# Attention block with modulated layer norm: scale product in three parts, last output columns gated on VectorE

## The chip, the cores and the metric

The kernel runs on one core of one Trainium2 chip. The metric is the device time of one execution in microseconds (us), as a median of several runs. The core's engines work side by side, each through its own queue in order: TensorE (PE in the profile; PEld are its weight loads), VectorE (DVE), ScalarE (ACT), GpSimd (POOL) and SyncE (SP), which here issues most DMAs. An engine starts an instruction when all that stands before it in its own queue is issued and the semaphores that it waits for are set.

## The reference

```python
B, N, D = (2, 256, 1152)
mod = (_silu(c) @ w_mod).reshape(B, 6, 1, D)
shift_a, scale_a, gate_a, shift_m, scale_m, gate_m = [mod[:, i] for i in range(6)]
h = _layernorm(x, axis=-1) * (1 + scale_a) + shift_a
qkv = h @ wqkv
q, k, v = (qkv[..., :D], qkv[..., D:2 * D], qkv[..., 2 * D:])
p = _softmax(jnp.einsum('bqd,bkd->bqk', q, k) * D ** (-0.5), axis=-1)
a = jnp.einsum('bqk,bkd->bqd', p, v) @ wo
return x + gate_a * a
```

All inputs are bf16. x is [2, 256, 1152], c [2, 1152], wqkv [1152, 3456], wo [1152, 1152], w_mod [1152, 6912], of which the first three sixths (shift, scale, gate) are used.

## The kernel before

The 512 tokens of both batches are four tiles of 128 (t = 0 to 3; two tiles a batch), and D is nine tiles of 128 (k). All weights are loaded once.

*Who sets the order.* `vec`, `sca`, `ten` and `spq` (L81 to L84) record each instruction for DVE, ACT, PE and SP; `pin` (L86) then fixes those four queues to the order in which the source calls them. POOL is not pinned. So a line moved in the source moves in its engine's queue, and everything behind it in that queue waits for it. All recorded instructions carry line 74; they are told apart by their tiles' names.

*Loads* (L149 to L164, all issued by SP): x tiles 1, 0, 3; the first CA = 384 columns of `wS` (scale) in five pieces; the first 1024 columns of K's first two weight slices; x tile 2; the third slice; the other 768 columns of `wS` in three pieces of 576 KB; the other slices of `wK` in four pieces; the left-over columns of the first three; `wH` (shift). The weights of Q, V, the gate (`wG`) and `wO` follow.

*Start of the work* (L342 on). Thirteen filler matmuls on `junk_ps` keep TensorE busy while the first tiles arrive. Tile 1's mean comes from DVE (`dve_stats`, `dve_aggr`), the others' from ACT (`act_mean`). `centre(t)` (L224, DVE) writes x less its mean to `xc`; `turned` (L228) transposes its 128-column blocks on TensorE into psum; `from_psum` copies them to `xnT`. The variance of tiles 0 and 2 comes from ACT (`act_var`), that of 1 and 3 from DVE's `bn_stats`. The 1/sigma of a token isn't applied here: POOL computes it (`var_eps` L211, `rstd_parts` L249) as three bf16 parts, TensorE turns and spreads it over the partitions (`rstd_turn`, `rstd_spread`), and it is multiplied in later.

*Scale.* `scale_A` (L282) multiplies silu(c) with the first three column tiles of `wS`, into `psS0` and `psSA`; `scale_B` (L289) does the other six, into `psSB`. Each runs over nine row blocks kk. DVE reads the result from psum into `s1p` and writes `hTs` = `xnT` times the scale (`scaled`, L306).

*K from the scaled rows.* Six psum banks `accs` collect six of K's nine output tiles. For k = 0, 1, 2 this is done piece by piece as tokens become ready (`k_part`, L309: batch 0 first, then tile 3, then tile 2), for k = 3 to 8 for all 512 tokens (`k_step`, L323, six matmuls each). Two more output tiles take their first three k in `early_half` (L316; psum tile `psE`), and the rest later. The small psum pools `psum_a` and `psum_b` have one bank each, which `psE`, `tp3`, `tp2`, `tp8`, `psSA`, `psSB`, `turn_ps` and `spread_ps` use in turn. `tp8` holds the ninth column blocks of tiles 3 and 2. After the K steps come the shift product (`shift_block`, `psH`), the rest of K, `hT` (`modulated`), Q, the scores, V (`v_group`), and attention times V.

*Gate.* DVE sums `gacc` over the rows of `wG`; POOL's all-reduce (L589) spreads it to `gate_bc`.

*Output.* For each token tile, chunks of 384 columns are multiplied by `wO` on TensorE; DVE multiplies by the gate (`ga`) and adds x (`o_sb`); SP stores the tile. The last tile's chunks are 384, 384, 192, 128 and 64 columns. For the last 192 columns POOL has multiplied `wO` by the gate ahead of time (`wo_last`, L610); DVE then adds only x to the 128, and for the last 64 TensorE adds x by a matmul with the identity, and ACT copies them out. The three stores of the last tile hold 768, 320 and 64 columns.

Of the kernel before, what the change touches and what calls it, by code (L numbers as in the profile page):

```python
# [8 lines left out]
ALU = mybir.AluOpType  # L9
# [7 lines left out]
def kernel(  # L17
# [22 lines left out]
    NEARLY = 2  # L40
    WE = (NACC + NEARLY) * P
    KA = 3
    KB = KT - KA
    NR = 54

    x_f = x.rearrange("b n d -> (b n) d")
# [94 lines left out]
    def load_mod(tile_, which, k0, k1, c0, c1):  # L141
        spq.dma_start(out=tile_[:, k0:k1, c0:c1], in_=wmod_v[:, k0:k1, which, c0:c1])

    def load_k(k0, k1, c0=0, c1=D):
        spq.dma_start(out=wK[:, k0:k1, c0:c1], in_=wqkv_v[:, k0:k1, D + c0 : D + c1])
# [9 lines left out]
    load_k(1, 2, 0, WE)  # L155
    load_x(2)
    load_k(2, 3, 0, WE)
    for k0 in range(0, KT, 3):
        load_mod(wS, 1, k0, k0 + 3, CA, D)
    for k0, k1 in ((3, 4), (4, 5), (5, 7), (7, 9)):  # L160
        load_k(k0, k1)
    load_k(0, KA, WE, D)
    for k0, k1 in PAIRS:
        load_mod(wH, 0, k0, k1, 0, D)  # L164
# [5 lines left out]
    def fillers(n):  # L170
        for _ in range(n):
            ten.matmul(junk_ps, lhsT=junk_rhs[:, 0:P], rhs=junk_rhs, start=True, stop=True)
# [18 lines left out]
    def sc_rhs(kk):  # L191
        return scT_rep[:, kk].rearrange("p r b -> p (r b)")
# [18 lines left out]
    def var_eps(t):  # L211
        nc.gpsimd.tensor_scalar(out=rstd[:, t : t + 1], in0=mv[:, t, 1:2], scalar1=1.0, scalar2=EPS,
                                op0=ALU.mult, op1=ALU.add)
# [10 lines left out]
    def centre(t, c0=0, c1=D):  # L224
        vec.tensor_scalar(out=xc[:, t, c0:c1], in0=x_sb[:, t, c0:c1], scalar1=mv[:, t, 0:1], scalar2=None,
                          op0=ALU.subtract)

    def turned(tp, cols):  # L228
        for j, (t, k) in enumerate(cols):
            ten.transpose(tp[:, j, :], xc[:, t, k * P : (k + 1) * P], ident)  # L230

    def tiles_of(t, k0, k1):
        return [(t, k) for k in range(k0, k1)]

    def from_psum(eng, t, k0, k1, tp, j0=0):
        dst, srct = xnT[:, k0:k1, t * P : (t + 1) * P], tp[:, j0 : j0 + k1 - k0, :]
        if eng is vec:
            vec.tensor_copy(out=dst, in_=srct)
        else:
            sca.copy(out=dst, in_=srct)  # L240
# [41 lines left out]
    def scale_A(kk):  # L282
        for j in range(KA):
            ten.matmul(
                psS0 if j == 0 else psSA[:, j - 1, :], lhsT=wS[:, kk, j * P : (j + 1) * P], rhs=sc_rhs(kk),
                start=False, stop=(kk == KT - 1), skip_group_check=True,
            )

    def scale_B(kk):  # L289
        for j in range(KA, KT):  # L290
            ten.matmul(
                psSB[:, j - KA, :], lhsT=wS[:, kk, j * P : (j + 1) * P], rhs=sc_rhs(kk),
                start=(kk == 0 and j == KA), stop=(kk == KT - 1), skip_group_check=True,
            )

    def shift_block(kk):
        for j in range(KT):
# [5 lines left out]
    def one(t):  # L303
        return slice(t * P, (t + 1) * P)
# [4 lines left out]
    def k_part(k, sl, first=False):  # L309
        for f in range(NACC):  # L310
            ten.matmul(
                accs[f][:, sl], lhsT=wK[:, k, f * P : (f + 1) * P], rhs=hTs[:, k, sl],
                start=first, stop=False, skip_group_check=True,
            )

    def early_half(k, b, ps):  # L316
        for i in range(NEARLY):
            ten.matmul(
                ps[:, i, :], lhsT=wK[:, k, (NACC + i) * P : (NACC + i + 1) * P], rhs=hTs[:, k, tok(b)],
                start=(k == 0 and i == 0), stop=(k == KA - 1), skip_group_check=True,  # L320
            )

    def k_step(k):  # L323
        for f in range(NACC):
            ten.matmul(
                accs[f], lhsT=wK[:, k, f * P : (f + 1) * P], rhs=hTs[:, k, :],
                start=False, stop=(k == KT - 1), skip_group_check=True,
            )
# [16 lines left out]
    dve_stats(1, 2)  # L345
    dve_aggr(1)
    centre(1)
    var_eps(1)
    act_mean(0)
    centre(0)  # L350
    act_mean(3)
# [8 lines left out]
    from_psum(vec, 1, KA, KT, tp1b)  # L360
    scale_A(0)
    scale_A(1)
    fillers(2)
    scale_A(2)
    scale_A(3)
    turned(tp0a, tiles_of(0, 0, KA))
    turned(tp0b, tiles_of(0, KA, KT))
    from_psum(vec, 0, 0, KA, tp0a)
    from_psum(sca, 0, KA, KT, tp0b)
    for kk in range(4, KT):  # L370
        scale_A(kk)
    act_var(0)
    centre(3, 0, CW)

    accs = [psum.tile([P, T], F32, tag="mm", name="acc") for _ in range(NACC)]
    scaled(0, tok(0), psS0[:, 0:1])
# [4 lines left out]
    psE = psum_a.tile([P, NEARLY, N], F32, tag="pa")  # L381
    k_part(0, tok(0), first=True)
    early_half(0, 0, psE)
    centre(3, CW, D)
    k_part(1, tok(0))
    act_mean(2)
    tp3 = bank(n=KT - 1, pool=psum_b, tag="pb")
    turned(tp3, tiles_of(3, 0, KT - 1))
    from_psum(vec, 3, 0, KA, tp3)
    from_psum(sca, 3, KA, KT - 1, tp3, KA)  # L390
    for k in range(KA):
        scaled(k, one(3), s1p[:, k, 1:2])
    centre(2)
    early_half(1, 0, psE)
    k_part(2, tok(0))
    k_part(0, one(3))
    k_part(1, one(3))
    act_var(2)
    tp2 = bank(n=KT - 1, pool=psum_b, tag="pb")
    turned(tp2, tiles_of(2, 0, KT - 1))  # L400
    k_part(2, one(3))
    early_half(2, 0, psE)
    sca.copy(out=early[:, :, tok(0)], in_=psE)
    from_psum(vec, 2, 0, KA, tp2)
    for k in range(KA):
        scaled(k, one(2), s1p[:, k, 1:2])
    from_psum(sca, 2, KA, KT - 1, tp2, KA)
    for s in range(NCH):
        dve_stats(3, s)
    dve_aggr(3)  # L410
    var_eps(3)
    for k in range(KA):
        k_part(k, one(2))
    psSB = psum_a.tile([P, KB, NR], F32, tag="pa")
    for kk in range(6):
        scale_B(kk)
    tp8 = bank(n=2, pool=psum_b, tag="pb")
    turned(tp8, [(3, KT - 1), (2, KT - 1)])
    from_psum(vec, 3, KT - 1, KT, tp8, 0)
    from_psum(vec, 2, KT - 1, KT, tp8, 1)  # L420
    rstd_parts()
    for kk in range(6, KT):
        scale_B(kk)
    vec.tensor_scalar_add(out=s1p[:, KA:KT, :], in0=psSB[:, :, 0:B], scalar1=1.0)
    for k in range(KA, KT):
        for b in range(B):
            scaled(k, tok(b), s1p[:, k, b : b + 1])
    psE = psum_b.tile([P, NEARLY, N], F32, tag="pb")
    for k in range(KA):
        early_half(k, 1, psE)  # L430
    sca.copy(out=early[:, :, tok(1)], in_=psE)


    k_step(KA)
    rstd_turn()
    k_step(KA + 1)
    rstd_spread()
    for k in range(KT):
        vec.tensor_tensor(out=xnT[:, k, :], in0=xnT[:, k, :], in1=rstd_bc, op=ALU.mult)
    for k in range(KA + 2, KT):  # L440
        k_step(k)
    for f in range(NACC):
        evac(1, qkT[:, KT + f, :], accs[f])
# [162 lines left out]
    LASTW = 64  # L606
    TAILW = CW // 2
    wo_last = const.tile([P, KT, TAILW], BF16)
    for k in range(KT):
        nc.gpsimd.tensor_tensor(out=wo_last[:, k, :], in0=wO[:, k, D - TAILW :],  # L610
                                in1=gate_bc[:, B - 1, D - TAILW :], op=ALU.mult)
    for b in range(B):
        for gi, dv0 in enumerate(range(0, KT, 2)):
            ndv = min(2, KT - dv0)
# [10 lines left out]
    for t in range(TT):  # L625
        b = t // NQ
        o_sb = work.tile([P, D], BF16, tag="o_sb")
        if t < TT - 1:
            chunks = [(oc * CW, CW) for oc in range(NCH)]
            dma_after = {NCH - 1: (0, D)}  # L630
        else:
            chunks = [(0, CW), (CW, CW), (2 * CW, CW - TAILW), (D - TAILW, TAILW - LASTW), (D - LASTW, LASTW)]
            dma_after = {1: (0, 2 * CW), 3: (2 * CW, CW - LASTW), 4: (D - LASTW, LASTW)}
        for ci, (c0, w_) in enumerate(chunks):
            cs = slice(c0, c0 + w_)
            last = (t == TT - 1) and (ci == len(chunks) - 1)
            pregated = (t == TT - 1) and c0 >= D - TAILW
            ps = psum.tile([P, w_], F32, tag="mm")
            if last:
                ten.matmul(ps, lhsT=ident, rhs=x_sb[:, t, cs], start=True, stop=False)  # L640
            for k in range(KT):
                ten.matmul(
                    ps, lhsT=attnT[:, k, t * P : (t + 1) * P],
                    rhs=(wo_last[:, k, c0 - (D - TAILW) : c0 - (D - TAILW) + w_] if pregated else wO[:, k, cs]),
                    start=(k == 0 and not last), stop=(k == KT - 1),
                )
            if last:
                sca.copy(out=o_sb[:, cs], in_=ps)
            elif pregated:
                vec.tensor_tensor(out=o_sb[:, cs], in0=ps, in1=x_sb[:, t, cs], op=ALU.add)  # L650
            else:
                ga = work.tile([P, CW], F32, tag="ga")
                vec.tensor_tensor(out=ga[:, :w_], in0=ps, in1=gate_bc[:, b, cs], op=ALU.mult)
                vec.tensor_tensor(out=o_sb[:, cs], in0=ga[:, :w_], in1=x_sb[:, t, cs], op=ALU.add)
            if ci in dma_after:
                d0, dw = dma_after[ci]
                dma_eng = nc.scalar if last else spq
                dma_eng.dma_start(out=out_f[t * P : (t + 1) * P, d0 : d0 + dw], in_=o_sb[:, d0 : d0 + dw])
# [35 lines left out]
```

## Time and profile before

| | us |
|---|---|
| median of 3 runs (lowest, highest) | 99.31 (99.2, 99.7) |
| the profiled execution's own time | 99.89 |
| its span, first to last recorded instruction | 98.2 |
| TensorE busy | 92.7 |
| VectorE busy | 71.0 |
| ScalarE busy | 34.0 |
| GpSimd busy | 26.3 |

The times that the prediction works with are those of the profiled execution, counted from its span's start. A row of the timeline gives the start, the time from the first start to the last end, the engine, the line, the operation, out<-in by the program's names, the shape, how many instructions the row merges, and in brackets the engine's idle time before the row and what ended it. A matmul's duration holds its way through the array as well; matmuls that follow each other start closer than their durations. The granted clock is 9 tenths or more in all 40 slices, and the DMA engines are busy for nine tenths or more from 2.5 us to 52 us, at 370 to 414 GB/s from 7 us on.

### The profile page before, as it was taken

How to read it: one execution, taken by the hardware profiler on the slowest of the kernel's cores; microseconds unless marked ns; L12 is line 12 of the kernel's file. 1: busy time of each engine (PE TensorE's matmuls, PEld its weight loads, DVE VectorE, ACT ScalarE, POOL GpSimd, SP SyncE). 2: the span in 40 equal slices, each digit the busy share in tenths (PEclk: the TensorE clock that was granted, in tenths of full speed). 3: DMA queues.
4: the chain of work that ended last, by engine and by line, in shares of the span. 5: the costliest groups of instructions: out<-in, count | busy, mean ns of one | idle time of the engine just before them, and what ended most of it. 6: DMA issues, size and time to landing. Idle time of an engine off the chain costs nothing.

```text
span 98.2 us, 1836 instructions
## 1 busy us (share of the span) xinstructions
PE 92.7 (94%) x739; PEld 56.1 (57%) x739; DVE 71.0 (72%) x137; ACT 34.0 (35%) x68; POOL 26.3 (27%) x32
## 2 busy tenths in 40 slices
PE   3999999989999999999999999999999999999970
PEld 1328888634466444444448765556678755556660
DVE  1487468846955899999991999991237667879870
ACT  5195985202290792233222436332126400000000
POOL 6042001820000000000000000008999970049800
PEclk9999999999999999999999999999999999999999
DMA  2999999999999999999998000000000000302113
GB/s 48 348 295 385 387 401 404 394 411 403 384 391 387 398 408 372 372 369 365 400 414 317 33 0 0 0 0 0 0 0 7 0 0 0 120 7 114 72 67 108
DMA packets 16488, 21.06 MB, mean 215 GB/s; under 512 B 1504, under 2 KB 10976, under 8 KB 16480
## 3 DMA queue, kind: packets, MB, share of 16 engines
q1 hardware_dynamic: 16064, 20.93, 58.4%
q8 instruction: 6, 0.10, 0.4%
q10 hardware_dynamic: 416, 0.02, 0.3%
q14 instruction: 2, 0.02, 0.0%
HBM read 19.76 MB, written 1.18 MB: 213 GB/s over the span
## 4 chain that ended last, share of the span: by engine, by line
PE 87%; DVE 5%; POOL 3%; issue 1%; DVEq 0%
PE ps L74 61%; PE acc L74 10%; PE junk_ps L74 6%; PE s_ps L74 4%; PE tp L74 2%; PE psH L74 2%; DVE stats L74 1%; POOL rstd L250 1%; DVE o_sb L74 1%; DVE hTs L74 1%; DVE ga L74 1%; PE psSA L74 1%; POOL parts L251 1%; POOL parts L253 1%; DVE junk_rhs L74 1%
## 5 line engine op out<-in xcount | busy, mean ns | idle before, releaser
L589 POOL PARTITION_ALL_REDUCE gate_bc<-gacc x2 | 13.7, 6886 | 46.4 <-DVE gacc L74 46.4
L74 DVE SCALAR_TENSOR_TENSOR gacc<-wG,scT_f,gacc 128x1152 f32<-128x1152 bf16 x16 | 22.7, 1417 | 0.5
L74 PE MATMUL ps<-wqv,hT 128*128 128x384 bf16 x108 | 17.9, 326 | 0.0
L74 PE MATMUL ps<-hT,wqv 128*128 128x512 bf16 x81 | 17.6, 379 | 0.0
L74 PE MATMUL ps<-wO,attnT 128*128 128x384 bf16 (+1 forms) x108 | 17.0, 319 | 0.0
L74 PEld LDWEIGHTS <-attnT 128*128 128x128 bf16 x126 | 11.3, 98 | 6.4
L74 PEld LDWEIGHTS <-hT 128*128 128x128 bf16 x108 | 10.5, 98 | 6.7
L74 PEld LDWEIGHTS <-wK 128*128 128x128 bf16 x123 | 10.1, 97 | 6.9 <-issue 1.1
L74 PE MATMUL acc<-hTs,wK 128*128 128x128 bf16 (+2 forms) x90 | 13.1, 294 | 0.6 <-DVE hTs L74 0.5
L74 PEld LDWEIGHTS <-wqv 128*128 128x128 bf16 x81 | 7.9, 98 | 9.6 <-DVE hT L74 0.4
L74 ACT CAST qkT<-ps 128x512 bf16<-128x512 f32 x10 | 5.8, 583 | 10.9 <-PE ps L74 10.9
L74 DVE TENSOR_TENSOR ga<-ps,gate_bc 128x384 f32<-128x384 f32 (+1 forms) x12 | 6.5, 539 | 3.5 <-PE ps L74 3.5
L74 PE MATMUL junk_ps<-junk_rhs 128*128 128x512 bf16 x15 | 6.3, 598 | 1.5 <-DVE junk_rhs L74 1.5
L610 POOL TENSOR_TENSOR wo_last<-wO,gate_bc 128x192 bf16<-128x192 bf16 x9 | 5.7, 667 | 6.8 <-issue 6.8
L74 ACT CAST v_sb<-ps 128x384 bf16<-128x384 f32 x10 | 4.7, 475 | 8.3 <-PE ps L74 8.2
L74 DVE TENSOR_TENSOR o_sb<-ga,x_sb 128x384 bf16<-128x384 f32 (+1 forms) x12 | 7.2, 601 | 0.4
L74 DVE TENSOR_TENSOR xnT<-xnT,rstd_bc 128x512 bf16<-128x512 bf16 x9 | 5.5, 684 | 2.1 <-ACT rstd_bc L74 2.1
L74 ACT CAST o_sb<-ps 128x64 bf16<-128x64 f32 x1 | 0.2, 213 | 17.3 <-PE ps L74 17.3
L74 PE MATMUL ps<-hTs,wK 128*128 128x512 bf16 x21 | 5.0, 378 | 0.0
L74 DVE CAST attnT<-ps 128x512 bf16<-128x512 f32 (+1 forms) x6 | 3.5, 602 | 1.8 <-PE ps L74 1.8
L74 DVE BATCH_NORM_STATS2 stats<-x_sb 128x6 f32<-128x384 bf16 x6 | 3.0, 548 | 2.2 <-DMA x_sb<-in_x_dram 2.2
L74 PEld LDWEIGHTS <-junk_rhs 128*128 128x128 bf16 x15 | 1.9, 138 | 4.5 <-issue 3.0
(86 smaller groups left out, 94.2 us busy)
## 6 DMA issues: line engine op xcount, KB each, us to landing
wqv<-in_wqkv_dram SPq DMA_DIRECT2D x5, 864.0 KB, 9.9
wG<-in_w_mod_dram SPq DMA_DIRECT2D x3, 864.0 KB, 9.6
wO<-in_wo_dram SPq DMA_DIRECT2D x3, 864.0 KB, 8.5
wH<-in_w_mod_dram SPq DMA_DIRECT2D x4, 576.0 KB, 10.0
wS<-in_w_mod_dram SPq DMA_DIRECT2D x3, 576.0 KB, 6.6
x_sb<-in_x_dram SPq DMA_DIRECT2D x4, 288.0 KB, 3.8
wK<-in_wqkv_dram SPq DMA_DIRECT2D x2, 576.0 KB, 10.4
wqv<-in_wqkv_dram SPq DMA_DIRECT2D x3, 288.0 KB, 8.7
```

The costliest lines, as they stand in the source:

```text
L74: r = fn(*a, **k)
L250: nc.gpsimd.tensor_tensor(out=rstd, in0=rstd, in1=neg_half, op=ALU.pow)
L251: nc.gpsimd.tensor_scalar(out=parts[:, :, 0], in0=rstd, scalar1=1.0, scalar2=None, op0=ALU.mult)
L253: nc.gpsimd.tensor_scalar(out=parts[:, :, 1], in0=rest, scalar1=1.0, scalar2=None, op0=ALU.mult)
L589: ar = nc.gpsimd.partition_all_reduce(gate_bc[:, b, :], gacc[:, b, :], P, bass.bass_isa.ReduceOp.add)
L610: nc.gpsimd.tensor_tensor(out=wo_last[:, k, :], in0=wO[:, k, D - TAILW :], in1=gate_bc[:, B - 1, D - TAILW :], op=ALU.mult)
```

## The change

- The other six column tiles of the scale product become two parts of three, `scale_part` into `psM` and `psL`; the second runs in the middle of `k_step(5)`, which is split in two. `wS` and `wK` are loaded in the matching order, five DMAs more.
- Parked steps stand elsewhere: tile 0's transposes ahead of `scale_A(2)`; one filler less; `early_half(1)` behind tile 2's transposes; `bn_stats` of tile 3 spread, one behind `centre(3)`, one ahead of `centre(2)`, one behind tile 2's `hTs`; `rstd_parts` right behind `var_eps`; `tp8` behind `k_step(3)`, the turn behind `k_step(4)`.
- `centre(3)` is one instruction for 1152 columns, where it was 384 and 768.
- `wo_last` is made by three DVE instructions of three row tiles each, in tile 1's part of the output loop. TensorE adds x for all of the last 192 columns, ACT copies them, and the last two stores are 192 columns each.

```diff
+    CM = KM * P
     for k0 in range(0, KT, 3):
-        load_mod(wS, 1, k0, k0 + 3, CA, D)
-    for k0, k1 in ((3, 4), (4, 5), (5, 7), (7, 9)):
-        load_k(k0, k1)
+        load_mod(wS, 1, k0, k0 + 3, CA, CM)
+    for k in range(KA, KM):
+        load_k(k, k + 1)
+    for k0 in range(0, KT, 3):
+        load_mod(wS, 1, k0, k0 + 3, CM, D)
+    for k in range(KM, KT):
+        load_k(k, k + 1)
...
-    def scale_B(kk):
-        for j in range(KA, KT):
...
+    def scale_part(ps, k0, kk):
+        for j in range(KA):
+            c0 = (k0 + j) * P
+            ten.matmul(
+                ps[:, j, :], lhsT=wS[:, kk, c0 : c0 + P], rhs=sc_rhs(kk),
+                start=(kk == 0 and j == 0), stop=(kk == KT - 1), skip_group_check=True,
+            )
+
+    def scaled_part(ps, k0):
+        vec.tensor_scalar_add(out=s1p[:, k0 : k0 + KA, :], in0=ps[:, :, 0:B], scalar1=1.0)
+        for k in range(k0, k0 + KA):
+            for b in range(B):
+                scaled(k, tok(b), s1p[:, k, b : b + 1])
...
-    var_eps(1)
...
-    fillers(2)
-    scale_A(2)
-    scale_A(3)
+    fillers(1)
     turned(tp0a, tiles_of(0, 0, KA))
     turned(tp0b, tiles_of(0, KA, KT))
...
-    for kk in range(4, KT):
+    for kk in range(2, KT):
         scale_A(kk)
     act_var(0)
-    centre(3, 0, CW)
...
-    centre(3, CW, D)
+    centre(3)
     k_part(1, tok(0))
     act_mean(2)
     tp3 = bank(n=KT - 1, pool=psum_b, tag="pb")
     turned(tp3, tiles_of(3, 0, KT - 1))
+    dve_stats(3, 0)
     from_psum(vec, 3, 0, KA, tp3)
...
-    centre(2)
-    early_half(1, 0, psE)
     k_part(2, tok(0))
     k_part(0, one(3))
     k_part(1, one(3))
+    dve_stats(3, 1)
+    centre(2)
     act_var(2)
     tp2 = bank(n=KT - 1, pool=psum_b, tag="pb")
     turned(tp2, tiles_of(2, 0, KT - 1))
...
+    k_part(2, one(3))
+    early_half(1, 0, psE)
+    early_half(2, 0, psE)
+    sca.copy(out=early[:, :, tok(0)], in_=psE)
     from_psum(sca, 2, KA, KT - 1, tp2, KA)
-    for s in range(NCH):
-        dve_stats(3, s)
+    dve_stats(3, 2)
     dve_aggr(3)
+    var_eps(1)
     var_eps(3)
+    rstd_parts()
     for k in range(KA):
         k_part(k, one(2))
...
+    psM = psum_a.tile([P, KA, NR], F32, tag="pa")
+    for kk in range(KT):
+        scale_part(psM, KA, kk)
+    scaled_part(psM, KA)
+    psE = psum_b.tile([P, NEARLY, N], F32, tag="pb")
+    for k in range(KA):
+        early_half(k, 1, psE)
+    sca.copy(out=early[:, :, tok(1)], in_=psE)
...
+    k_step(KA)
     tp8 = bank(n=2, pool=psum_b, tag="pb")
     turned(tp8, [(3, KT - 1), (2, KT - 1)])
...
+    k_step(KA + 1)
     rstd_turn()
-    k_step(KA + 1)
+    k_step(KA + 2, 0, NACC // 2)
     rstd_spread()
+    psL = psum_b.tile([P, KA, NR], F32, tag="pb")
+    for kk in range(KT):
+        scale_part(psL, KM, kk)
+    scaled_part(psL, KM)
+    k_step(KA + 2, NACC // 2, NACC)
     for k in range(KT):
         vec.tensor_tensor(out=xnT[:, k, :], in0=xnT[:, k, :], in1=rstd_bc, op=ALU.mult)
-    for k in range(KA + 2, KT):
+    for k in range(KM, KT):
         k_step(k)
...
-    for k in range(KT):
-        nc.gpsimd.tensor_tensor(out=wo_last[:, k, :], in0=wO[:, k, D - TAILW :],
-                                in1=gate_bc[:, B - 1, D - TAILW :], op=ALU.mult)
+    def gated_columns(k0, k1):
+        vec.tensor_tensor(
+            out=wo_last[:, k0:k1, :], in0=wO[:, k0:k1, D - TAILW :], op=ALU.mult,
+            in1=gate_bc[:, B - 1, D - TAILW :].unsqueeze(1).to_broadcast([P, k1 - k0, TAILW]),
+        )
...
-            dma_after = {1: (0, 2 * CW), 3: (2 * CW, CW - LASTW), 4: (D - LASTW, LASTW)}
+            dma_after = {1: (0, 2 * CW), 2: (2 * CW, CW - TAILW), 4: (D - TAILW, TAILW)}
...
-            if last:
+            if pregated:
                 ten.matmul(ps, lhsT=ident, rhs=x_sb[:, t, cs], start=True, stop=False)
...
-            if last:
+            if pregated:
                 sca.copy(out=o_sb[:, cs], in_=ps)
-            elif pregated:
-                vec.tensor_tensor(out=o_sb[:, cs], in0=ps, in1=x_sb[:, t, cs], op=ALU.add)
...
+            if t == NQ - 1:
+                gated_columns(3 * ci, 3 * ci + 3)
```

More of the change, by code (lines that the diff above doesn't have):

```diff
@@ L42 @@
     KA = 3
-    KB = KT - KA
+    KM = 2 * KA
     NR = 54
@@ L287, in scale_A @@
             )
-    def scale_B(kk):
-        for j in range(KA, KT):
+    def scale_part(ps, k0, kk):
+        for j in range(KA):
+            c0 = (k0 + j) * P
             ten.matmul(
-                psSB[:, j - KA, :], lhsT=wS[:, kk, j * P : (j + 1) * P], rhs=sc_rhs(kk),
-                start=(kk == 0 and j == KA), stop=(kk == KT - 1), skip_group_check=True,
-            )
+                ps[:, j, :], lhsT=wS[:, kk, c0 : c0 + P], rhs=sc_rhs(kk),
+                start=(kk == 0 and j == 0), stop=(kk == KT - 1), skip_group_check=True,
+            )
+    def scaled_part(ps, k0):
[3 more added lines that the diff above has]
+                scaled(k, tok(b), s1p[:, k, b : b + 1])
     def shift_block(kk):
@@ L321, in early_half, with k_step @@
             )
-    def k_step(k):
-        for f in range(NACC):
+    def k_step(k, f0=0, f1=NACC):
+        for f in range(f0, f1):
             ten.matmul(
@@ L388 @@
     turned(tp3, tiles_of(3, 0, KT - 1))
+    dve_stats(3, 0)
     from_psum(vec, 3, 0, KA, tp3)
-    from_psum(sca, 3, KA, KT - 1, tp3, KA)
     for k in range(KA):
         scaled(k, one(3), s1p[:, k, 1:2])
-    centre(2)
-    early_half(1, 0, psE)
+    from_psum(sca, 3, KA, KT - 1, tp3, KA)
     k_part(2, tok(0))
@@ L400 @@
     turned(tp2, tiles_of(2, 0, KT - 1))
-    k_part(2, one(3))
-    early_half(2, 0, psE)
-    sca.copy(out=early[:, :, tok(0)], in_=psE)
     from_psum(vec, 2, 0, KA, tp2)
@@ L406 @@
         scaled(k, one(2), s1p[:, k, 1:2])
+    k_part(2, one(3))
+    early_half(1, 0, psE)
+    early_half(2, 0, psE)
+    sca.copy(out=early[:, :, tok(0)], in_=psE)
     from_psum(sca, 2, KA, KT - 1, tp2, KA)
-    for s in range(NCH):
-        dve_stats(3, s)
+    dve_stats(3, 2)
     dve_aggr(3)
+    var_eps(1)
     var_eps(3)
+    rstd_parts()
     for k in range(KA):
         k_part(k, one(2))
[L414 to L427, printed above, removed]
+    psM = psum_a.tile([P, KA, NR], F32, tag="pa")
+    for kk in range(KT):
+        scale_part(psM, KA, kk)
+    scaled_part(psM, KA)
     psE = psum_b.tile([P, NEARLY, N], F32, tag="pb")
@@ L434 @@
     k_step(KA)
+    tp8 = bank(n=2, pool=psum_b, tag="pb")
+    turned(tp8, [(3, KT - 1), (2, KT - 1)])
+    from_psum(vec, 3, KT - 1, KT, tp8, 0)
+    from_psum(vec, 2, KT - 1, KT, tp8, 1)
+    k_step(KA + 1)
     rstd_turn()
-    k_step(KA + 1)
+    k_step(KA + 2, 0, NACC // 2)
     rstd_spread()
+    psL = psum_b.tile([P, KA, NR], F32, tag="pb")
[3 more added lines that the diff above has]
+    k_step(KA + 2, NACC // 2, NACC)
     for k in range(KT):
         vec.tensor_tensor(out=xnT[:, k, :], in0=xnT[:, k, :], in1=rstd_bc, op=ALU.mult)
-    for k in range(KA + 2, KT):
+    for k in range(KM, KT):
         k_step(k)
@@ L644 @@
                     rhs=(wo_last[:, k, c0 - (D - TAILW) : c0 - (D - TAILW) + w_] if pregated else wO[:, k, cs]),
-                    start=(k == 0 and not last), stop=(k == KT - 1),
+                    start=(k == 0 and not pregated), stop=(k == KT - 1),
                 )
-            if last:
+            if pregated:
                 sca.copy(out=o_sb[:, cs], in_=ps)
-            elif pregated:
-                vec.tensor_tensor(out=o_sb[:, cs], in0=ps, in1=x_sb[:, t, cs], op=ALU.add)
             else:
```

## The prediction

> **What bounds the kernel now.** I read the page's busy shares and chain first, then the timeline of the first 32 us, then that of the last 20, then the DMA view in narrow windows.
>
> ```profile
> PE 92.7 (94%) x739; PEld 56.1 (57%) x739; DVE 71.0 (72%) x137; ACT 34.0 (35%) x68; POOL 26.3 (27%) x32
> ...
> PE 87%; DVE 5%; POOL 3%; issue 1%; DVEq 0%
> ```
>
> TensorE (PE) is busy for 92.7 of 98.2 us. 1.5 us lie before its first matmul and 3.1 after its last (95.09), so all its waits between come to under 1 us of modelled idle. The chain agrees. From 22.19 on the timeline shows no PE gap up to 95.09, so an edit there pays only by the work it takes off PE, and the early edits pay only through PE's gaps before 22.19. (Starts follow each other at a steady pitch without a wait: about 0.025 us at 54 columns, 0.056 at 128, 0.109 at 256, 0.216 at 512. A gap below is a start later than that pitch gives.)
>
> ```profile
> 8.08 0.59 PE L74 MATMUL junk_ps<-junk_rhs 128*128 128x512 bf16 x2
> ...
> 10.04 0.81 PE L74 MATMUL acc<-hTs,wK 128*128 128x256 bf16 x6 [0.33 <-DVE hTs L74]
> ...
> 12.21 0.36 DVE L74 COPY xnT<-tp 128x384 bf16<-128x384 bf16 x1 [1.31 <-PE tp L74]
> ...
> 12.61 0.58 DVE L74 TENSOR_SCALAR hTs<-xnT,s1p 128x128 bf16<-128x128 bf16 x3
> ...
> 13.10 0.51 DVE L74 TENSOR_SCALAR xc<-x_sb,mv 128x1152 bf16<-128x1152 bf16 x1
> ...
> 13.67 0.62 PE L74 MATMUL tp<-ident,xc 128*128 128x128 bf16 x8
> ...
> 15.03 1.17 PE L74 MATMUL acc<-hTs,wK 128*128 128x128 bf16 x18 [0.18 <-DVE hTs L74]
> ...
> 15.22 1.47 DVE L74 BATCH_NORM_STATS2 stats<-x_sb 128x6 f32<-128x384 bf16 x3
> ...
> 17.19 0.63 PE L74 MATMUL psSB<-scT_rep,wS 128*128 128x54 bf16 x18
> ...
> 18.60 1.46 PE L74 MATMUL acc<-hTs,wK 128*128 128x512 bf16 x6
> ...
> 20.04 0.22 POOL L254 TENSOR_TENSOR parts<-rest,parts 128x4 bf16<-128x4 f32 x1
> ...
> 20.31 0.22 PE L74 MATMUL turn_ps<-ident,parts 128*12 128x128 bf16 x1 [0.26 <-POOL parts L254]
> ```
>
> What to see, as PE's gaps in order: 0.49 before 10.04 (the first `hTs`, behind the end of scale_A); 0.35 before 15.03 (`hTs` of tile 2); 0.13 before 17.19 (the last third of `wS`: issued at 8.31, 8.8 us to landing, so 17.1); 0.26 before 18.60 (`hTs` of k=3); 0.42 before 20.31 (POOL's `parts`). Tile 2's transposes (13.67) start just as centre(2) ends on VectorE (DVE), 13.10 + 0.51: PE has no slack there, DVE is the pace.
>
> ```profile
> 94.18 0.56 DVE L74 TENSOR_TENSOR o_sb<-ga,x_sb 128x384 bf16<-128x384 f32 x1
> 94.64 0.19 PE L74 MATMUL ps<-x_sb,ident 128*128 128x64 bf16 x1
> 94.66 0.35 DVE L74 TENSOR_TENSOR ga<-ps,gate_bc 128x192 f32<-128x192 f32 x1
> 94.67 0.43 PE L74 MATMUL ps<-wo_last,attnT 128*128 128x64 bf16 x9
> 95.05 0.36 DVE L74 TENSOR_TENSOR o_sb<-ga,x_sb 128x192 bf16<-128x192 f32 x1
> 95.13 0.21 ACT L74 CAST o_sb<-ps 128x64 bf16<-128x64 f32 x1 [17.26 <-PE ps L74]
> 95.32 0.28 DVE L74 TENSOR_TENSOR o_sb<-ps,x_sb 128x128 bf16<-128x128 f32 x1
> ```
>
> The end: DVE's last add ends at 95.60, SP issues 80 KB at 95.63, which lands 1.6 later, at 97.2; the span ends 0.95 after that.
>
> **The change, part by part.** I walk PE and DVE in the new order with the old durations; in the built program each queue stands as the source has it. Hand-overs from the rows: DVE to PE 0.053 (9.99 to 10.04), PE to DVE 0.037 (12.18 to 12.21).
>
> *Start.* One filler less is one pitch: 0.215. scale_A(2), (3) only move behind tile 0's transposes; PE's sum is otherwise the same, and every `wS` piece they need lands by 8.6, before they run at 8.8 to 9.3. Tile 0's transposes go from 8.66 to 8.29, after centre(0) (7.66). The first `hTs` waits for psS0 alone, so it and the first `acc` come 0.215 earlier (9.83).
>
> *centre(3) in one piece, bn_stats(3,0).* These stand in DVE's wait of 1.31 before 12.21, used to 11.25 where tile 3's copy can start at 12.00: free. If that cover went, PE would wait up to one bn pitch, 0.46.
>
> *early_half(1) taken from behind tile 3's transposes.* It covered `hTs`. Transposes from 11.35, copy 12.00 to 12.36, first `hTs` ready 12.65 + 0.05; PE is done with k_part(2) at 12.48: new gap 0.22.
>
> *bn_stats(3,1) ahead of centre(2).* Queued behind it are centre(2), tile 2's copy and its `hTs`, and PE waits for each. One bn pitch is 0.46 (three in 1.47 with a tail of 0.09). centre(2) moves to 13.35, ends 13.86, transposes at 13.91 (new gap 0.53). From there the old distance holds (13.67 to 15.03 is 1.36): k_part on tile 2 at 15.27, 0.24 **later** than before. The gap before it shrinks to 0.13, because early_half(1) and (2) now stand there. k_parts end at 16.27 (was 16.03).
>
> *Scale in parts.* 27 + 27 matmuls for 54, at 0.0253: the same 1.37. Psum hand-overs (`early`'s copy, tile 2's copy on ScalarE, ACT) end by 15.9 and 16.5, before 16.27 and 16.95. psM runs 16.27 to 16.95, then early_half covers; k_step(3) follows psM's last start by the same 0.965 as in before (17.63 to 18.60), so it starts at 17.90 and its gap of 0.26 stays. The landing of `wS` no longer waits: its middle columns are half the bytes. wK's third slice lands 11.2; 864 KB more at the 1.43 to 1.46 per 576 KB seen are 13.4, with the third piece's 1.6 of lateness 15.0, against 16.27. The last columns, behind three 288 KB slices of wK (0.74 each), come by 19.4, needed at 21.8. So SP's five more issues (0.4 to 0.5 each, under 0.74 of transfer) cost nothing; wH, 4 us ahead of its use, hides the rest.
>
> *POOL.* Aggregation ends at 16.27 (was 16.96), so `parts` is ready at 19.57. The turn now follows k_step(3), tp8 and k_step(4), at 20.60: the gap of 0.42 goes. What is late next is the third scale part: turn, half of k_step(5) to 21.40, spread to 21.81, psL to 22.50; `hTs` of k=6 is due 0.965 after psL's last start, 23.44, and the other half of k_step(5) covers only to 23.14: new gap 0.30. var_eps(1) moves in the source only; POOL's order in the program is unchanged. The moved tp8 has its psum bank free at 18.4.
>
> Then 18 x 0.216 = 3.89: shift starts at **27.33**, against 27.38. Checked by gaps: 0.24 late at 16.27; from there 0.13 and 0.42 go and 0.30 comes, 0.25 won back. The early stage is a draw, 0.05 gained by the walk. DVE ends its `xnT` products at 29.5 instead of 28.4, still ahead of its next input (29.79).
>
> *Gated columns.* POOL's nine (0.667 each) go; DVE gets three of 576 elements. Nearest rows: `xnT`<-`xnT`,`rstd_bc` (bf16 by f32 from SBUF, 512) 0.684, and `p_f` with a broadcast operand (512) 0.69, so 0.75 each by 1.04 ns an element. Bounds: 0.68 from below; from above twice the slope, 1.36, or POOL's 2.0. I take 0.75. Queued behind them are `ga`, `o_sb` of tiles 1 and 2. DVE's spare per chunk is 0.39 (1.465 of PE less 1.075): it is 1.0 late at most, PE has six banks, and DVE is level again by the last tile. `gate_bc` is ready at 80.4. Cost: nothing.
>
> *End.* DVE's last add goes to TensorE (one matmul more, 0.056, ahead of ACT's copy only). SP's last issue follows `o_sb` at 95.41, ACT's follows 95.40: 95.43, for 48 KB each, between rows of 16 KB (1.5) and 80 KB (1.6): landing 96.98, not 97.22: **0.24** gained. [...] Both stores have rows of 384 bytes. [...]
>
> **Sum:** 0.05 + 0.24 = 0.29 off the profiled execution (99.89, span 98.17): 99.60. That execution is 0.58 above the runs' median of 99.31; I take the same difference off the median: **99.0**.
>
> **Rivals.** (1) *Faster, 98.7.* In this trace the 13 fillers ran at 0.435, twice the later pitch. If the clock turns faster sooner in a timed run, PE and DVE start up to 0.77 earlier. Before can pass on only 0.42 of that (the `parts` gap), since psSB's last third waits for the landing at 17.1; the new order passes it all, less 0.18 because tile 0's transposes then wait for centre(0). That is 0.17 more, 98.83; each 0.1 by which `wS` lands later than here costs before alone another 0.1: 98.7 at 0.13. For: the runs are 0.2 to 0.7 under the profiled one. Against: a start up to 0.4 earlier gives nothing extra. 0.28. [...]
> (2) *Slower, 100.1.* The gated columns run at twice the slope, 1.36. DVE is then 3 x 1.28 - 7 x 0.39 = 1.1 late at the last 384 columns. It decides from 0.99 an instruction. Against: both rows near 0.69. 0.08.
> (3) *Slower, 99.8.* DVE is the early stage's bound and its four new or shifted hand-overs (after tp3, tp2, psM, psL) each cost 0.2 more than the rows. For: PE waits for DVE at all four. Against: the same kinds of hand-over are measured. 0.09.
> (4) *The POOL wait isn't there in timed runs*, so removing it pays nothing: +0.42, 99.4. Against: its chain stands 0.42 late. 0.05.
>
> **Chances.** Forecast 0.50. About 0.5% is what a measurement of this kernel can tell: 98.8 to 99.8. Faster: rival 1, 0.28. Slower: 0.08 for (2), half of (3), 0.02 of the forecast's spread: 0.15. Same: the rest, 0.57. The range takes (1) with `wS` up to 0.4 late, (3) and (4), and leaves out (2): 98.4 to 99.8.
>
> **What would show it.** Right: tile 2's transposes at 13.9 behind a PE gap of 0.5 released by DVE `xc`; no gap at the turn; a gap near 0.3 between the halves of k_step(5) and k=6; shift at 27.3; gated columns at 0.75; two last stores issued near 95.4. Wrong: shift before 26.8 or after 27.8, a PE gap after 28 us, or DVE late at the last tile.

## The result and the profile after

The changed kernel takes 106.09 us (median of 4 runs, 105.88 to 106.62) against 99.5 for the kernel before measured beside it: a ratio of 1.0701, 95% interval 1.0618 to 1.0784. It is 7% slower, where the forecast was 99.0 and the range ended at 99.8. The profiled execution took 106.62, its span 104.9. Some executions ran over 1.5% longer than the fastest of their kernel (one of the kernel before took 100.75, the first profiled one of e6 below 101.2); the ratios are of the means of the others, and the early stage of e6 is read from a second profile, e6b.

The page of the changed kernel: busy times, the granted clock by slices, and the chain that ended last.

```profile
PE 94.4 (90%) x734; PEld 57.8 (55%) x739; DVE 71.6 (68%) x139; ACT 34.4 (33%) x69; POOL 19.8 (19%) x23
...
PEclk9999557999999999999999999999999999999999
...
PE 81%; issue 10%; DVE 5%; POOL 1%; POOLq 0%
```

TensorE has hardly more to do than before (94.4 against 92.7, of which a slow stretch is part), but the chain now holds 10% of "issue", 1% before: time in which an engine waited for nothing that the profile shows. The clock has two slices of 5 tenths. The chain in order of time says where:

```profile
1.19 9.49 issue
10.68 0.28 POOL ident L100
10.96 0.49 POOL ones_row L109
...
11.49 0.24 PE psSA L74
```

GpSimd does six short memsets, then nothing for 9.5 us, and only then makes `ident` and `ones_row`, which the first matmuls after the fillers need. The timeline of GpSimd (POOL) and TensorE over the same stretch, with the idle time and its end in brackets:

```profile
10.68 0.28 POOL L100 TENSOR_SCALAR_AFFINE_SELECT ident<-ident 128x128 bf16<-128x128 bf16 x1 [9.55 <-issue]
...
11.49 0.24 PE L74 MATMUL psSA<-ones_row,ones_bf 1*128 1x108 bf16 x1 [4.43 <-POOL ones_row L109]
11.72 1.14 PE L74 MATMUL tp<-ident,xc 128*128 128x128 bf16 x9
...
15.75 1.41 PE L74 MATMUL acc<-hTs,wK 128*128 128x256 bf16 x6 [0.30 <-DVE hTs L74]
```

And the busy times in two stretches (core time, PE, PEld, DVE, ACT and POOL busy; the last three columns are granted clock, DMA share and GB/s):

```profile
0.00:12.00 12.00, 6.06 (x18) 2.23 (x19) 3.77 (x10) 4.80 (x9) 1.80 (x10) 0.92 0.86 287
12.00:17.00 5.00, 4.70 (x53) 3.94 (x51) 2.86 (x10) 2.45 (x4) 1.64 (x4) 0.50 1.07 385
```

TensorE idles for 4.4 us, and the clock granted afterwards is 0.50 up to 17 us: nine transposes take 1.14 where they took 0.68. Nothing in the early order that the prediction walked through moved by such an amount. The same row of the kernel before, and a later one of its GpSimd rows, tell what is different:

```profile
1.41 0.29 POOL L100 TENSOR_SCALAR_AFFINE_SELECT ident<-ident 128x128 bf16<-128x128 bf16 x1 [0.29 <-POOL ones_bf L107]
...
87.15 5.72 POOL L610 TENSOR_TENSOR wo_last<-wO,gate_bc 128x192 bf16<-128x192 bf16 x9 [6.79 <-issue]
```

There too GpSimd waits for nothing that is shown, 6.79 us long, but at the end, behind its all-reduces and ahead of its first plain product. In the built programs GpSimd has a separate instruction at these places, which the profile doesn't show: ahead of L100 and ahead of the first all-reduce in both kernels, and in the kernel before also ahead of L610, where the change removes it with the nine products.

**Theory L (library).** An assumption, made from the two idle stretches above (6.79 and 9.55 us); no row shows a load. GpSimd would hold the code either of its plain operations or of the all-reduce, changing it would cost 6 to 10 us, and what an execution leaves loaded would be what the next one finds. In the kernel before, the nine products would then force the change back, hidden in an idle stretch; the changed kernel ends on the all-reduce, so the change would fall at the start of the next execution, ahead of everything. **Rivals:** O, the new order of the early stage holds GpSimd back; G, the gated columns cost the time on VectorE.

### The profile page after: what moved, and what is told of

Same layout as the page of the kernel before. It is cut to its first block, busy times and chain, and to the rows that moved or that the text cites. A ratio compares the mean times of both kernels' runs of the same rounds, so it can differ in the third digit from the quotient of the medians.

```text
span 104.9 us, 1827 instructions
## 1 busy us (share of the span) xinstructions
PE 94.4 (90%) x734; PEld 57.8 (55%) x739; DVE 71.6 (68%) x139; ACT 34.4 (33%) x69; POOL 19.8 (19%) x23
## 4 chain that ended last, share of the span: by engine, by line
PE 81%; issue 10%; DVE 5%; POOL 1%; POOLq 0%
PE ps L74 57%; PE acc L74 11%; PE s_ps L74 4%; PE tp L74 3%; PE psH L74 2%; DVE hTs L74 2%; PE psSA L74 1%; DVE o_sb L74 1%; DVE ga L74 1%; PE psL L74 1%; PE psM L74 1%; PE psE L74 1%; POOL ones_row L109 0%; PE psS L74 0%; DVE stats L74 0%
## 5 line engine op out<-in xcount | busy, mean ns | idle before, releaser
L74 PE MATMUL acc<-hTs,wK 128*128 128x128 bf16 (+2 forms) x88 | 13.8, 301 | 0.9 <-DVE hTs L74 0.6
L74 DVE COPY xnT<-tp 128x384 bf16<-128x384 bf16 (+2 forms) x7 | 2.3, 347 | 8.7 <-PE tp L74 8.7
L74 DVE TENSOR_TENSOR o_sb<-ga,x_sb 128x384 bf16<-128x384 f32 (+1 forms) x12 | 6.5, 541 | 0.4
L74 ACT CAST o_sb<-ps 128x128 bf16<-128x128 f32 (+1 forms) x2 | 0.5, 238 | 17.0 <-PE ps L74 17.0
L74 ACT COPY xnT<-tp 128x640 bf16<-128x640 bf16 (+1 forms) x3 | 2.2, 729 | 7.5 <-PE tp L74 6.5
```

The lines of the kernel that those rows point to most:

```text
L74: r = fn(*a, **k)
```

## The experiments

**e1.** The changed kernel and one plain GpSimd operation behind the all-reduces:

```diff
     wo_last = const.tile([P, KT, TAILW], BF16)
+    pool_last = const.tile([P, 1], F32)
+    nc.gpsimd.tensor_tensor(out=pool_last, in0=gate_bc[:, B - 1, 0:1], in1=gate_bc[:, B - 1, 0:1], op=ALU.mult)
```

> The changed kernel with one more instruction: a GpSimd product of 128x1 behind the two all-reduces, its output unused. Theory L (library): GpSimd holds the code of the plain operations or that of the all-reduce, and what an execution leaves loaded is what the next one finds. Then the switch back falls behind the all-reduces (6.8 us idle there, as in the kernel before), GpSimd's first AFFINE_SELECT starts near 1.4 us instead of 10.7, PE's wait of 4.4 us ahead of psSA goes, and the time is that of the prediction's walk, 98.8 to 99.5. Rival O (order): the new order of the early stage holds GpSimd back; then nothing changes, 106. Rival G: the gated columns on VectorE cost the time; 106 too.

Measured: 100.14 against 99.65, ratio 1.0039 (1.0011 to 1.0067). GpSimd's rows:

```profile
1.41 0.29 POOL L100 TENSOR_SCALAR_AFFINE_SELECT ident<-ident 128x128 bf16<-128x128 bf16 x1 [0.29 <-POOL ones_bf L107]
66.35 13.69 POOL L601 PARTITION_ALL_REDUCE gate_bc<-gacc  x2 [47.44 <-DVE gacc L74]
87.00 0.18 POOL L622 TENSOR_TENSOR pool_last<-gate_bc 128x1 f32<-128x1 f32 x1 [6.97 <-issue]
```

One instruction of 0.18 us, whose output nobody reads, takes 6 us off the kernel: the idle time moves from the start (9.55) to the end (6.97), where no engine waits for GpSimd. O and G fall as the cause, since the new order and VectorE's gated columns (0.75 each) are still there. But 100.14 is above theory L's 98.8 to 99.5: something else costs 0.4%.

**e2.** The kernel before with the gated columns alone on VectorE (the nine GpSimd products replaced by `gated_columns`).

> The kernel before with one part of the change: the last 192 columns of Wo gated by three VectorE instructions, GpSimd's nine left out; x is added and stores are made as before. Theory L: the all-reduce is now GpSimd's last operation, so the start stalls: 105 to 107, first AFFINE_SELECT near 10.7 us. Rival O: the early order is as before, so 99.3 to 99.8. Rival G: slower, but with the loss in the output loop and none at the start.

Measured: 105.84, ratio 1.0605 (1.055 to 1.0659). This part alone brings nearly the whole loss, with the early order untouched:

```profile
10.65 0.28 POOL L100 TENSOR_SCALAR_AFFINE_SELECT ident<-ident 128x128 bf16<-128x128 bf16 x1 [9.52 <-issue]
```

**e3.** The reverse: the changed kernel with GpSimd's nine products back.

> The changed kernel with that one part undone: GpSimd gates the last columns in nine instructions as before, all else as changed. Theory L: 98.8 to 99.5, first AFFINE_SELECT near 1.4 us. Rival O: 106. Rival G: 99 as theory L says, but then the first AFFINE_SELECT has to stay near 10.7 us.

Measured: 100.03, ratio 1.0034 (1.0011 to 1.0058); AFFINE_SELECT starts at 1.41, with the idle time again at the end (7.46 ahead of `wo_last`). The time is above the 98.8 to 99.5 that was expected, as in e1.

**e4.** The changed kernel with a plain copy in the place of each all-reduce:

```diff
-        ar = nc.gpsimd.partition_all_reduce(gate_bc[:, b, :], gacc[:, b, :], P, bass.bass_isa.ReduceOp.add)
+        ar = nc.gpsimd.tensor_scalar(out=gate_bc[:, b, :], in0=gacc[:, b, :], scalar1=1.0, scalar2=None, op0=ALU.mult)
```

> The changed kernel with the sum over partitions left out: GpSimd copies gacc to gate_bc with a plain operation, so the gate is not summed and no all-reduce is called. Theory L: no other code is ever loaded, so the start is free and the time 98.8 to 99.6, though GpSimd's last plain operation is not where the kernel before has it. If what counts were only a GpSimd instruction at the place of wo_last, or the early order (rival O), the start would still stall, 106.

Measured: 100.24, ratio 1.0057 (1.0032 to 1.0083), again above what was expected (98.8 to 99.6). The start is free:

```profile
1.16 0.29 POOL L100 TENSOR_SCALAR_AFFINE_SELECT ident<-ident 128x128 bf16<-128x128 bf16 x1
```

AFFINE_SELECT has no wait ahead of it, although the built program keeps its separate instruction there. It isn't the place of `wo_last` that counts: where no all-reduce is ever called, the start is free. Since the stalled instruction stands ahead of the execution's own all-reduce, and one instruction behind the all-reduces takes the stall away (e1), I take it to be owed from the execution before. With e1 to e4 theory L is shown as far as runs can: the stall comes and goes with what GpSimd does last, 9.55 and 9.52 us where that is the all-reduce (the changed kernel, e2), none where it is a plain operation (AFFINE_SELECT at 1.41 in before, e1 and e3, at 1.16 in e4). That the wait is a load of code is a reading; the runs show when it is owed and how long it is.

**e9.** How the loss divides: 34 fillers for 13 in the changed kernel.

> The changed kernel with 34 fillers at the start instead of 13, so that TensorE works on until GpSimd has its code (10.7 us). Theory L with the slow clock as its second half: the wait itself (4.3 us) stays, but the fillers keep the clock at full pitch, so tile 1's transposes run at 0.056 instead of 0.103 and 1.7 to 2.4 us come back: 103.6 to 104.6. If the whole loss is the wait alone, the time stays at 106.

Measured: 104.11, ratio 1.0422 (1.0378 to 1.0466).

```profile
11.21 0.22 PE L74 MATMUL psSA<-ones_row,ones_bf 1*128 1x108 bf16 x1
11.38 0.68 PE L74 MATMUL tp<-ident,xc 128*128 128x128 bf16 x9
...
13.80 0.81 PE L74 MATMUL acc<-hTs,wK 128*128 128x256 bf16 x6 [0.33 <-DVE hTs L74]
```

TensorE starts the real work nearly as late as in the changed kernel (11.21 against 11.49), but at full pitch (nine transposes in 0.68 us, 1.14 there), and its first `acc` follows after 2.6 us, not 4.3. (GpSimd's wait is 8.88 here and `ones_row` is ready at 10.78, so the fillers themselves hold TensorE for the last 0.4.) Beside e3, whose fillers ran equally long, the changed kernel has psSA 4.34 later (7.15 to 11.49), the second `acc` group 6.60 (10.62 to 17.22) and the shift 6.61 (27.37 to 33.98): 4.3 us of wait and 2.3 in the stretch at a granted clock of 0.50 behind it.

**e8.** How long GpSimd idles between a plain operation and an all-reduce while the DMA engines work: a small all-reduce and a plain product in the kernel before, behind the parts.

```diff
-    rstd_parts()
+    parts_done = rstd_parts()
+    load_a = const.tile([P, 8], F32)
+    load_b = const.tile([P, 1], F32)
+    early_ar = nc.gpsimd.partition_all_reduce(load_a[:, 0:TT], rstd, P, bass.bass_isa.ReduceOp.add)
+    tc.add_manual_dep(early_ar.ins, parts_done.ins.name, SCHED, reason="behind parts")
+    nc.gpsimd.tensor_tensor(out=load_b, in0=load_a[:, 0:1], in1=load_a[:, 1:2], op=ALU.mult)
```

> The kernel before with a small all-reduce (128x4) and a small plain product behind it on GpSimd, right behind the parts at 20 us, where GpSimd has nothing else to do until 66 us and the DMA engines are nine tenths busy; their outputs are unused. Theory L with the loads slowed by other DMA traffic: each change of code costs about 9.5 us here, as at the changed kernel's start, against 6.8 to 7.0 behind the all-reduces, where the DMA engines are idle. Rival: a change costs the same anywhere, about 7, and the 2.7 us more at the start come from something else there. The kernel's time should not move, 99.2 to 100.

```profile
26.63 2.18 POOL L424 PARTITION_ALL_REDUCE load_a<-rstd  x1 [6.29 <-issue]
36.15 0.32 POOL L426 TENSOR_TENSOR load_b<-load_a 128x1 f32<-128x1 f32 x1 [7.33 <-issue]
```

6.29 us idle ahead of the all-reduce and 7.33 ahead of the plain product behind it, in one execution of 100.23 us (expected 99.2 to 100). My theory that other DMA traffic makes the stretch longer falls: at that time (the kernel before has a DMA share of 1.06 from 20 to 36 us) it is no longer than behind the gate's all-reduces (6.79 in before, 7.46 in e3), and where the start's other 1.5 to 2.2 us come from (8.88 to 9.55 there) stays open.

**The rest of the change, part by part.** e1 and e3 are still 0.4% slower than before, e4 0.6%. e5 is the kernel before with the end alone changed, e6 with the early stage alone.

> The kernel before with the change of the end alone: TensorE adds x for all of the last 192 columns, ScalarE copies them, the last two stores are 192 columns each; GpSimd gates as before. Prediction's theory: the last SP store is issued 0.2 us earlier and the time falls by 0.24 (0.2%). Rival, from the traces of e1 and e3: PE's extra matmul moves the end by 0.056 and ScalarE's 48 KB store takes 1.7 to 1.8 us to land instead of 1.5 for 16 KB, so it is 0.05 to 0.15 us slower, last PE start to span end 3.34 instead of 3.27.

Measured e5: 99.76 against 99.78, ratio 1.0005 (0.9985 to 1.0025). The rows of e3's last stores (KB each, us to landing):

```profile
out_dram<-o_sb ACTq DMA_DIRECT2D x1, 48.0 KB, 1.8
out_dram<-o_sb SPq DMA_DIRECT2D x1, 48.0 KB, 1.6
```

SP does issue its last store earlier, but the two stores start together, and one of them takes 1.8 us to land (ScalarE's in e3, SP's in e5), where before had 1.5 for 16 KB and 1.6 for 80 KB. No gain is left that these runs can tell.

> The kernel before with the change of the early stage alone: scale in parts, loads, parked steps, centre(3); gate, x and stores as before. Prediction's theory: a draw, within 0.1 us, shift starting within 0.1 us of before where the fillers ran equally long. Rival: in timed runs the early stage costs 0.2 to 0.4 us, since e1 and e3 are 0.4 us slower than before and the end explains only 0.1.

Measured e6: 100.19 against 99.78, ratio 1.0041 (1.0015 to 1.0067). So the 0.4% is the early stage. Where it arises is looked for in e6b, a second profile of e6, beside b2, a second profile of the kernel before:

> e6 unchanged, for a profile without the disturbance of the first: by the walk shift starts at 27.0 to 27.4, within 0.1 us of before with equally long fillers. If it starts 0.3 us or more later than before does at the same filler time, the early part's 0.4% is in the trace.

> The kernel before, unchanged, for a second profile: does the last third of wS land near 17.1 us again, and does a start earlier than in the first profile pass on less than itself? By rival 1 of the prediction it does not pass on more than 0.42. If wS lands clearly earlier here, psSB does not wait and shift starts before 27.0.

b2 (99.43 us):

```profile
9.64 0.82 PE L74 MATMUL acc<-hTs,wK 128*128 128x256 bf16 x6 [0.33 <-DVE hTs L74]
...
18.32 1.46 PE L74 MATMUL acc<-hTs,wK 128*128 128x512 bf16 x5
19.70 0.22 PE L74 MATMUL turn_ps<-ident,parts 128*12 128x128 bf16 x1
...
26.77 1.08 PE L74 MATMUL psH<-scT_rep,wH 128*128 128x54 bf16 x36
```

e6b (99.77 us):

```profile
9.48 0.81 PE L74 MATMUL acc<-hTs,wK 128*128 128x256 bf16 x6 [0.33 <-DVE hTs L74]
...
13.57 0.62 PE L74 MATMUL tp<-ident,xc 128*128 128x128 bf16 x8 [0.39 <-DVE xc L74]
...
23.23 4.04 PE L74 MATMUL acc<-hTs,wK 128*128 128x512 bf16 x18 [0.34 <-DVE hTs L74]
27.11 1.07 PE L74 MATMUL psH<-scT_rep,wH 128*128 128x54 bf16 x36
```

e5, which has the early stage of before, waits for `wS` itself:

```profile
17.26 0.63 PE L74 MATMUL psSB<-scT_rep,wS 128*128 128x54 bf16 x18 [0.58 <-DMA wS<-in_w_mod_dram]
```

What to see: from the first `acc` to the shift the new order needs 17.62 to 17.64 in every profile at full clock (e1, e3, e4, e6, e6b, e9). The old order needs 17.13 in b2, 17.34 in the first profile of before, 17.40 in e2, 17.42 in e8 and 17.63 in e5. In b2 the turn comes 1.38 after k_step(3)'s start, about the 1.29 of its six matmuls: the wait of 0.42 for `parts`, which the prediction credited, isn't there, nor in e5 (1.38 too); in e2 and e8 it is. The new order pays its waits for VectorE every time; what it takes away is there in some executions only.

The profiles don't show the 0.41% itself. b2 and e6b differ by 0.34, but e5 and e6b, whose fillers ran equally long (4.70 and 4.68), by 0.01: their shifts start at 27.12 and 27.11. Overall, the shift starts at 27.38, 26.77, 27.12 and 27.47 in the old order (before, b2, e5, e8) and at 27.37, 27.06, 27.18 and 27.11 in the new (e3, e1, e4, e6b), 27.2 on average in both. What differs in the timed runs stays open; which steps cost it, e7 tells.

**e7.** e6 with two steps back in place:

```diff
+    early_half(1, 0, psE)
     k_part(2, tok(0))
     k_part(0, one(3))
     k_part(1, one(3))
-    dve_stats(3, 1)
     centre(2)
+    dve_stats(3, 1)
...
-    early_half(1, 0, psE)
     early_half(2, 0, psE)
```

> e6 with two steps put back: centre(2) ahead of bn_stats(3,1) on VectorE, and early_half(1) behind tile 3's transposes. If VectorE's order is what costs the early stage its gaps (0.25, 0.55 and 0.13 us in e3), the gap ahead of tile 2's transposes goes and shift starts 0.4 to 0.5 us earlier than in e6: 0.4 us faster than e6. If wK or POOL's parts bind instead, it is level with e6, with a new gap at k_step(3) or at the turn.

Measured: 99.6 against 99.78, ratio 0.9982 (0.996 to 1.0003), 0.6 us under e6. From first `acc` to shift it takes 17.17 (9.63 to 26.80), 0.46 less, one bn pitch: tile 2's transposes, which wait for VectorE's `xc` in e6b (13.57, 0.39 idle), follow without a wait at 13.26. So the two steps together cost what the early stage had lost; the pitch points to VectorE's order, but they were not put back one by one.

**e10.** e7 with more of TensorE's work behind the two products whose `hTs` it waits for:

```diff
-    for k in range(KA):
+    for k in range(KA - 1):
         k_part(k, one(2))
...
     scaled_part(psM, KA)
+    k_part(KA - 1, one(2))
...
-    k_step(KA + 2, 0, NACC // 2)
+    k_step(KA + 2, 0, 2)
...
-    k_step(KA + 2, NACC // 2, NACC)
+    k_step(KA + 2, 2, NACC)
```

> e7 with two covers made longer: k_part(2) of tile 2 behind psM instead of ahead of it (0.34 us), and k_step(5) split 2 + 4 instead of 3 + 3 (0.22 us). If PE's gaps ahead of k_step(3) and k=6 (0.28 each in e7) are waits for VectorE's hTs alone, both go nearly whole and it is 0.4 to 0.5 us faster than e7: 99.0 to 99.3, 0.5% under before. If DMA landings bind instead, it is level with e7.

Measured: 98.94 against 99.85, ratio 0.992 (0.9894 to 0.9947). Both gaps (0.28 each in e7) close, and the shift comes 16.68 after the first `acc`:

```profile
9.55 0.82 PE L74 MATMUL acc<-hTs,wK 128*128 128x256 bf16 x6 [0.33 <-DVE hTs L74]
...
16.89 1.46 PE L74 MATMUL acc<-hTs,wK 128*128 128x512 bf16 x5
...
26.23 1.07 PE L74 MATMUL psH<-scT_rep,wH 128*128 128x54 bf16 x36
```

This version, with scale in three parts, GpSimd's gating and the old end, beats both kernels.

## Why the prediction was wrong

- **The step that failed: "*Gated columns.* POOL's nine (0.667 each) go ... Cost: nothing."** VectorE's side of it held: 0.75 an instruction, as forecast, and level by the last tile. What was priced at nothing is the removal: with the nine products GpSimd's idle stretch ahead of them went (6.79 in before), and one of 9.55 came at the start of the execution (9.52 in e2, where this part stands alone and 6.2 of it reach the end). No rival had it; rival 2 looked for the loss on VectorE. The page of before showed the price, 6.8 us of GpSimd idle ahead of `wo_last` ended by "issue", and I read it as idle time of an engine that nobody waits for. The rows show such stretches of 6.29 to 7.7 inside an execution and 8.88 to 9.55 at the start; that what GpSimd does last decides whether the start has one, e1, e2 and e4 show.
- **The start and the queues behind it.** The walk's gaps stood where it put them: in e3 tile 2's transposes start at 13.84 (forecast 13.91), behind VectorE's `xc`; k=6 waits behind half of k_step(5); no gap is at the turn; the shift starts at 27.37 (27.33). Against the first profile of before (27.38) the draw is exact.
- **"The early stage is a draw": in the profiles, not in the timed runs,** where e6 loses 0.41%. The gaps credited to the change, 0.13 for `wS` and 0.42 for `parts`, are there in some executions of the kernel before only (`parts` in three of five profiles). That was rival 4, priced at 0.42 and given 0.05; e6's 0.41% is of its size, but that it is the same loss isn't shown. Rival 1 took the start wrongly. Its bound for before, 0.42, doesn't hold: fillers 1.21 shorter in b2 start the shift 0.61 earlier. And the new order doesn't pass a shorter start on: with fillers 1.04 shorter in e6b and 1.39 in e1 than in e3, the shift starts 0.26 and 0.31 earlier, because TensorE then waits for VectorE's `xc` ahead of tile 1's transposes (0.50 in e6b). Its argument that before waits for the landing does hold in e5, where `wS` lands at 17.2 (issued 7.89, 9.3 to landing).
- **"0.24 gained" at the end** was mis-sized: 0.0, within 0.15 of gain and 0.25 of loss (e5). The two stores of 48 KB were priced at 1.55 each; issued together, they take 1.6 and 1.8. That they hold each other up is my estimate from these figures, not shown.
- The cost of "five more issues" was right: in e3 and e6b TensorE waits for no landing.

## What to carry to other kernels

Before the last GpSimd instruction of its kind is moved or dropped, ask what GpSimd does last without it. This kernel mixes plain GpSimd operations with the all-reduce: ending on the all-reduce it takes 106.09 us, and with one throwaway plain instruction of 0.18 us behind it 100.14 (e1); in a kernel like it, try to end on the kind that it starts with. An idle stretch ended by "issue" can hide a cost: here the edit removed the instruction behind one of 6.79 us, and one of 9.55 came elsewhere. A wait that one profile shows is credited in full only if a second profile shows it too (0.42 for `parts`: three of five profiles), while the steps put into VectorE's queue, for which TensorE waits, were paid in each of the six profiles (17.62 to 17.64 from the first `acc` to the shift, 17.17 with two steps put back, e7).

## What the runs showed of the hardware

- What GpSimd does last in this kernel decides whether its start stalls: 9.55 and 9.52 us behind the all-reduce (the changed kernel, e2), nothing behind a plain operation (e1, e4). That loaded code outlives an execution is theory L, an assumption that no row shows. No run shows what an execution of another kernel would find. GpSimd's idle stretch between the two kinds is 6.29 and 7.33 us amid full DMA traffic (e8), 6.8 to 7.7 with hardly any (before, where the DMA share is 0.10 from 80.4 to 88 us, e1, e3, b2), and 8.88 to 9.55 at an execution's start (e9, e2, the changed kernel); the reason for the last difference is open.
- An idle TensorE paid twice in the changed kernel: 4.43 us without a matmul, then a granted clock of 0.50 from 12 to 17 us, 2.3 us more. With fillers through the wait the granted clock was 0.997 over the whole execution (e9), 0.967 in the changed kernel.
- The same 13 fillers took 5.73 us in the first profile of the kernel before and 4.52 in the second (b2). From the first filler's start to that of `psSA` behind them it is 0.435 and 0.342 a filler, where the later pitch is 0.216. The granted clock reads 1.00 through the first (0 to 8 us) and 0.996 over the whole of b2, so that a clock turns fast there, and at a moment that varies, as rival 1 assumes, is an estimate from their pace alone; no row shows what sets it, and the prediction had one run only.
